# Chunk attention, Fourier mixing and an MLP on one core: pairs of batches in turn, or one batch at a time threaded through the MLP

## The chip, the cores and the metric

One core of a Trainium2 chip runs one program. Its engines work side by side, each through its own instructions in order: TensorE (PE in the rows; its weight loads are PEld), VectorE (DVE), ScalarE (ACT), GpSimd (POOL) and SyncE (SP), which here only issues DMAs. The metric is the time of one execution in microseconds of device time. TensorE's clock has two levels, 1.2 and 2.4 GHz; the profile tells the granted clock of a stretch as a share of the higher.

## The reference

Attention inside chunks of 64 tokens, then an FNet block: the real part of a Fourier transform over sequence and width is added to x, the sum u is normalised, and a two-layer MLP of the normalised rows is added back to u.

```python
# q, k, v: (8 batches, 8 heads, 576 tokens, 64), float32
scores = scale * np.matmul(q_c, k_c.transpose(0, 1, 2, 4, 3))   # chunks of 64
attn = np.exp(scores - max); attn = attn / (sum + 1e-09)
x = np.matmul(attn, v_c)        # -> (8, 576, 512) after the heads are joined
mixed = np.real(np.fft.fft(np.fft.fft(x, axis=1), axis=2))
u = x + mixed
un = (u - mean(u)) / np.sqrt(var(u) + 1e-06)
out = u + np.maximum(un @ w_ch1, 0.0) @ w_ch2      # 512 -> 2048 -> 512
```

The two weight matrices come as float64, and the kernel rounds them to float32 on the chip.

## The kernel before, in words

4608 rows make 36 tiles of 128 rows. A batch has nine chunks: four tiles of two chunks each (two of low chunks, `LO`, two of high ones, `HI`), and a middle chunk; the middle chunks of two batches share a tile (`RE`, "rest"). So the kernel works in four pairs of batches, nine tiles each.

A generator `attention(pr)` gives the attention of a pair in small steps, four to a tile: `att_S` (scores and their softmax, L215), `att_T` (transposes of q and k of the next tile, L197), `att_V` (probabilities times v, L252) and `att_P` (transposes of the probabilities, L246). `shift` (L282) moves single rows between tiles by DMA, `fold` (L296) adds and subtracts the low and high halves on GpSimd, which halves the Fourier work. `post(pr)` is the rest: the sequence transform (`z`, L368 and L378, into `zf`), the width transform (`mix`, L410) with u and its mean and variance (L423 to L429), the normalising (`un`, L440) and its transposes (`unT`), and the MLP in three groups of three tiles, 384 columns: `up` (L483) with the relu into `h` on ScalarE (L490), then `dn` (L501), the sum `o` (L512) and the store. TensorE takes a float32 matmul as two instructions, so that up is 128 instructions to a group and dn 96.

The order is written out by hand in the loop at the end. Attention of the first pair runs alone, with a weight piece rounded at every second step. Then `post` of a pair runs, and the steps of the next pair's attention are dealt out among its MLP steps, from the ninth step of `post` on; the Fourier part and the normalising of a pair stand between the MLPs of two pairs. A weight piece (32 of them, 128x512 float64, 512 KB) is rounded by seven operations on VectorE and a product on GpSimd (`round_weight`, L170), in place in one of two `raw` buffers; the load of piece i+2 is issued after the product of piece i. All DMAs are issued by SP, in order; a transfer's issue waits until the transfer eight before it has landed.

Of the kernel before, what the change touches and what calls it, by code (L numbers as in the profile page):

```python
# [16 lines left out]
def kernel(  # L17
# [45 lines left out]
    G = 3  # L63
    NG = NT // G
# [3 lines left out]
    in_p = ctx.enter_context(tc.tile_pool(name="in", bufs=3))  # L68
    one_p = ctx.enter_context(tc.tile_pool(name="one", bufs=1))
    two_p = ctx.enter_context(tc.tile_pool(name="two", bufs=2))  # L70
    sm_p = ctx.enter_context(tc.tile_pool(name="sm", bufs=4))
    x_p = ctx.enter_context(tc.tile_pool(name="x", bufs=2 * NT))
    pm_p = ctx.enter_context(tc.tile_pool(name="pm", bufs=2 * NM + 1))
# [6 lines left out]
    eps = const.tile([128, 1], FP32, name="eps")  # L80
    tk = const.tile([128, NM + 1, 2, NQ], FP32, name="tk")
# [5 lines left out]

    LO, HI, RE = "lo", "hi", "rest"
    order = [(RE, 0, 0)] + [(what, b, i) for b in range(2) for what in (LO, HI) for i in range(NM)]

    def kind(n):
        return order[n % NT][0]

    def chunks(n):

        pr, n0 = divmod(n, NT)
        what, b, i = order[n0]
        b += 2 * pr
        if what == RE:
            return [(2 * pr, NC // 2), (2 * pr + 1, NC // 2)]  # L100
# [7 lines left out]
    xs, pms = {}, {}  # L108

    def load(n):  # L110
        for src, dst, nm in ((q, qs, "q"), (k, ks, "k")):
            t = two_p.tile([128, H, D], FP32, tag=nm, name=nm)
            (b0, c0), (b1, c1) = chunks(n)
            if b0 == b1 and c1 == c0 + 1:
                parts = [(0, 128, b0, c0)]
            else:
                parts = [(0, CH, b0, c0), (CH, CH, b1, c1)]
            for p0, np_, b, c in parts:
                nc.sync.dma_start(
                    out=t[p0:p0 + np_], in_=src[b, :, c * CH:c * CH + np_, :].rearrange("h p d -> p h d")  # L120
                )
            dst[n] = t
        t = in_p.tile([128, 2, NJ, D], FP32, tag="v", name="v")
        for i, (b, c) in enumerate(chunks(n)):
            for e in range(2):
                nc.sync.dma_start(
# [5 lines left out]
    def load_tables():  # L132
# [4 lines left out]
        t = one_p.tile([128, NM + 1, 2, NQ], FP32, tag="big", name="seq")  # L137
# [3 lines left out]
        for r0 in (0, CH):  # L141
            nc.sync.dma_start(out=t[r0:r0 + 1, NM], in_=seq_tab[0:1, 0])
            nc.sync.dma_start(out=t[r0 + 1:r0 + CH, NM], in_=seq_tab[1:CH, NM])
        a, b = tk.rearrange("p i r f -> p (i r) f"), t.rearrange("p i r f -> p (i r) f")
# [4 lines left out]
        nc.sync.dma_start(out=cd, in_=dim_tab[:, 0:2, 0:HM + 1])  # L149
        nc.sync.dma_start(out=cs[:, HM + 1:DM], in_=dim_tab[:, 2, 1:HM])  # L150
        nc.sync.dma_start(out=sd, in_=dim_tab[:, 3, 1:HM])
        nc.gpsimd.memset(cs[:, 0:HM + 1], 0.0)
        nc.sync.dma_start(out=cs[0:1, 0:HM + 1], in_=dim_tab[0:1, 2, 0:HM + 1])
        nc.gpsimd.memset(cs[0:1, HM + 1:DM], 0.0)
# [6 lines left out]
    raws = {}  # L161

    def load_weight(i):

        if i < len(pieces):
            t = two_p.tile([128, 512, 2], U32, tag="raw", name="raw")
            nc.sync.dma_start(out=t.rearrange("p f r -> p (f r)"), in_=pieces[i][1].bitcast(U32))
            raws[i] = t

    def round_weight(i):  # L170

        if i >= len(pieces):
            return
        w, t = pieces[i][0], raws.pop(i)
        lo, hi, wi = t[:, :, 0], t[:, :, 1], w.bitcast(U32)
# [65 lines left out]
    def att_P(n):  # L245
        ex = es.pop(n)  # L246
        pt = turn(lambda j: ex[:, j].rearrange("p e k -> p (e k)"))
        t = two_p.tile([128, NJ, 128], FP32, tag="pT", name="pT")
# [3 lines left out]
    def att_V(n):  # L252
# [13 lines left out]
        x = x_p.tile([128, DM + 1], FP32, tag="x", name="x")  # L266
# [11 lines left out]
        xs[n] = x  # L278

    def tile_of(pr, what, b=0, i=0):  # L280
        return pr * NT + order.index((what, b, i))

    def shift(pr, b):

        lows = [xs[tile_of(pr, LO, b, i)] for i in range(NM)]
        r = b * CH
        rest = xs[tile_of(pr, RE)][r:r + 1, 0:DM]
        t = one_p.tile([2 * NM + 1, DM], FP32, tag="first", name="first")
        for i in range(NM):
            nc.sync.dma_start(out=t[2 * i:2 * i + 2], in_=lows[i][0:CH + 1:CH, 0:DM])  # L290
        nc.sync.dma_start(out=t[2 * NM:2 * NM + 1], in_=rest)
        for i in range(NM):
            nc.sync.dma_start(out=lows[i][0:CH + 1:CH, 0:DM], in_=t[2 * i + 1:2 * i + 3])
        nc.sync.dma_start(out=rest, in_=t[0:1])

    def fold(pr, b, i):  # L296

        pm = pm_p.tile([128, 2, HM], FP32, tag="pm", name="pm")
        if i == NM and b == 1:
            pms[pr, 1, NM] = pms[pr, 0, NM]  # L300
            return
        if i == NM:
            s = xs[tile_of(pr, RE)]
        else:
            s = sums[i]
            low, high = xs[tile_of(pr, LO, b, i)], xs[tile_of(pr, HI, b, i)]
            nc.gpsimd.tensor_tensor(out=s[:, 0:DM], in0=low[:, 0:DM], in1=high[:, 0:DM], op=ALU.add)
        near, far = s[:, 0:HM], s[:, DM:HM:-1]
        nc.gpsimd.tensor_tensor(out=pm[:, 0], in0=near, in1=far, op=ALU.add)
        if i < NM:  # L310
            near, far = far, near
        nc.gpsimd.tensor_tensor(out=pm[:, 1], in0=near, in1=far, op=ALU.subtract)
        mid = sm_p.tile([128, 1], FP32, tag="mid", bufs=2 * NM + 1, name="mid")
        nc.gpsimd.tensor_copy(mid, s[:, HM:HM + 1])
        pms[pr, b, i] = pm, mid

    def ready(pr, n):

        for b in range(2):
            for i in range(NM):  # L320
                if n == tile_of(pr, HI, b, i):
                    fold(pr, b, i)
            if n == tile_of(pr, LO, 1, NM - 1):
                fold(pr, b, NM)

    sums = [const.tile([128, DM + 1], FP32, name=f"sum{i}") for i in range(NM)]

    def attention(pr):

        first, last = pr * NT, (pr + 1) * NT - 1  # L330
        if pr == 0:
            load(0)
            load(1)
            load_tables()
            att_T(0)
        for n in range(first, last + 1):
            att_S(n)
            yield
            if n + 1 < NP * NT:
                att_T(n + 1)  # L340
            yield
            if n > first:
                att_V(n - 1)
                for b in range(2):
                    if n - 1 == tile_of(pr, LO, b, NM - 1):
                        shift(pr, b)
            if n + 2 < NP * NT:
                load(n + 2)
            yield
            att_P(n)  # L350
            ready(pr, n - 1)
            yield
        att_V(last)
        ready(pr, last)
# [3 lines left out]
    def post(pr):  # L358
        n0 = pr * NT
        zf = one_p.tile([128, 2, 4, NZ], FP32, tag="big", name="zf")  # L360
        for b in range(2):
            ins = [(*pms[pr, b, i], slice(0, 128), i) for i in range(NM)]
            ins.append((*pms[pr, b, NM], slice(b * CH, (b + 1) * CH), NM))
            for T in range(4):
                z = ps_f.tile([128, 512], FP32, tag="ff", name="z")
                fold_, half = T // 2, slice(T % 2 * 128, (T % 2 + 1) * 128)
                for pm, mid, p, i in ins:
                    nc.tensor.matmul(  # L368
                        out=z[:, 0:NQ],
                        lhsT=pm[p, fold_, half],  # L370
                        rhs=tk[p, i, fold_, :],
                        start=(i == 0),
                        stop=(i == NM),
                        skip_group_check=(T == 2),
                    )
                if T == 2:
                    for pm, mid, p, i in ins:
                        nc.tensor.matmul(  # L378
                            out=z[0:1, 0:NQ],
                            lhsT=mid[p],  # L380
                            rhs=tk[p, i, 0, :],
                            start=(i == 0),
                            stop=(i == NM),
# [214 lines left out]
```

## Time and profile before

| | |
|---|---|
| median of 3 runs | 1448.37 us (1448.15 to 1448.52) |
| profiled execution | 1449.68 us, its span 1447.9 us |
| mean granted clock | 0.935 |
| TensorE busy | 1287.3 us, 89% of the span |
| VectorE, ScalarE, GpSimd busy | 26%, 14%, 9% |
| read, written | 46.50 MB, 9.44 MB |

The page divides the span into 40 slices of 36.2 us and gives the busy tenths of each engine in each. In the chain that ended last, each step is followed back to what released it. A row of the chain is its start, its length and what ran. "x16" counts instructions that were merged into one row.

### The profile page before, as it was taken

The numbers are of one execution on the slowest core, as the hardware profiler recorded it, in microseconds if no ns is written. First come the engines' busy times: TensorE is split into PE (matmuls) and PEld (weight loads), VectorE is DVE, ScalarE is ACT, GpSimd is POOL, SyncE is SP. The second block draws the span as 40 slices with busy tenths as digits, with TensorE's granted clock in tenths as the row PEclk, the third lists the DMA queues.
The fourth block names the chain that finished last, engine by engine and source line by source line (L and its number), as shares of the span: only waits on it lengthen the run. The fifth ranks groups of instructions, "written<-read, shape, count | busy, mean of one in ns | idle before, by whom it ended". The sixth has DMA issues, their size and how long they took to land.

```text
span 1447.9 us, 14315 instructions
## 1 busy us (share of the span) xinstructions
PE 1287.3 (89%) x6000; PEld 698.2 (48%) x6000; DVE 381.4 (26%) x727; ACT 204.4 (14%) x443; POOL 131.2 (9%) x170
## 2 busy tenths in 40 slices
PE   3235859899999969999999959999999969999998
PEld 3223436455455446455455436455455435455553
DVE  3788687421111051121111051121111050000000
ACT  2010112012021022112021012112021011011010
POOL 0134122101001020001001020000001010000000
PEclk9556669999999989999999979999999989999999
DMA  6464224121110100021110101011100000000000
GB/s 155 103 148 108 73 69 121 45 52 28 39 45 15 37 15 22 15 52 25 42 44 16 37 15 23 15 38 37 39 14 7 16 1 0 10 13 8 15 0 22
DMA packets 126262, 57.03 MB, mean 39 GB/s; under 512 B 116533, under 2 KB 117046, under 8 KB 126198
## 3 DMA queue, kind: packets, MB, share of 16 engines
q1 hardware_dynamic: 126198, 56.13, 16.1%
q8 instruction: 47, 0.77, 0.2%
q14 instruction: 17, 0.14, 0.0%
HBM read 46.50 MB, written 9.44 MB: 39 GB/s over the span
## 4 chain that ended last, share of the span: by engine, by line
PE 81%; DVE 8%; issue 3%; POOL 3%; ACT 2%; DMA 2%; SPq 1%; POOLq 0%; DVEq 0%
PE up L483 35%; PE dn L501 34%; PE z L368 4%; PE pt L194 4%; POOL x L423 2%; PE xp L259 1%; PE sc L221 1%; PE mix L410 1%; DVE bst L425 1%; PE z L378 1%; DVE w L182 1%; DMA k<-in_k_dram 1%; DVE w L180 1%; DVE y L418 1%; DVE raw L186 1%
## 5 line engine op out<-in xcount | busy, mean ns | idle before, releaser
L483 PE MATMUL up<-unT,w 128*128 128x384 f32 x1536 | 517.1, 493 | 2.7 <-ACT unT L456 2.0
L501 PE MATMUL dn<-w,h 128*128 128x512 f32 x1152 | 504.5, 594 | 0.0
L483 PEld LDWEIGHTS up<-unT,w 128*128 128x128 f32 x1536 | 289.9, 192 | 196.4 <-issue 7.5
L501 PEld LDWEIGHTS dn<-w,h 128*128 128x128 f32 x1152 | 215.6, 190 | 256.0 <-issue 253.1
L490 ACT ACTIVATE h<-up 128x384 f32<-128x384 f32 x192 | 94.3, 491 | 512.0 <-PE up L483 512.0
L512 DVE TENSOR_TENSOR o<-dn,x 128x512 f32<-128x512 f32 x36 | 24.9, 692 | 396.7 <-PE dn L501 396.7
L230 DVE TENSOR_REDUCE mx<-sc 128x8 f32<-128x512 f32 x36 | 24.7, 687 | 242.7 <-PE sc L221 242.7
L194 PE MATMUL pt<-ident,q 128*128 128x128 f32 x144 | 27.1, 321 | 65.9 <-DMA q<-in_q_dram 65.9
L368 PE MATMUL z<-tk,pm 128*128 128x289 f32 (+1 forms) x192 | 69.5, 493 | 5.2 <-DVE zf L389 3.8
L194 PE MATMUL pt<-ident,un 128*128 128x128 f32 x144 | 25.4, 329 | 51.4 <-DVE un L440 49.4
L194 PEld LDWEIGHTS pt<-ident,q 128*128 128x128 f32 x144 | 20.5, 165 | 75.4 <-issue 72.8
L187 POOL TENSOR_TENSOR w<-w,raw 128x512 f32<-128x512 f32 x32 | 41.6, 1301 | 152.3 <-DVE raw L186 152.3
L268 DVE TENSOR_TENSOR x<-xp,rd 128x512 f32<-128x512 f32 x36 | 24.8, 690 | 115.5 <-PE xp L259 115.5
L368 PEld LDWEIGHTS z<-tk,pm 128*128 128x128 f32 (+1 forms) x192 | 35.5, 212 | 39.9 <-issue 28.0
L194 PEld LDWEIGHTS pt<-ident,un 128*128 128x128 f32 x144 | 20.2, 169 | 57.7 <-issue 41.7
L211 DVE COPY kT<-pt 128x512 f32<-128x512 f32 x36 | 24.5, 682 | 86.5 <-PE pt L194 86.5
L249 ACT COPY pT<-pt 128x512 f32<-128x512 f32 x36 | 21.1, 586 | 174.2 <-PE pt L194 174.2
L423 POOL TENSOR_TENSOR x<-y,x 128x513 f32<-128x513 f32 x16 | 27.4, 1711 | 189.6 <-DVE y L418 189.6
L440 DVE TENSOR_SCALAR un<-x,st,rstd 128x512 f32<-128x512 f32 x36 | 19.1, 558 | 94.3 <-PE pt L194 94.3
L238 ACT ACTIVATE ex<-ex 128x512 f32<-128x512 f32 x36 | 22.7, 629 | 143.9 <-DVE ex L232 143.9
L221 PE MATMUL sc<-kT,qT 64*64 64x64 f32 x1152 | 27.2, 237 | 14.9 <-ACT qT L204 13.6
L386 ACT COPY zf<-z 128x289 f32<-128x289 f32 x32 | 12.9, 402 | 183.2 <-PE z L368 151.0
(67 smaller groups left out, 682.1 us busy)
## 6 DMA issues: line engine op xcount, KB each, us to landing
raw<-in_moe_w_ch_dram SPq DMA_DIRECT2D x32, 512.0 KB
v<-in_v_dram SPq DMA_DIRECT2D x144, 64.0 KB
q<-in_q_dram SPq DMA_DIRECT2D x40, 128.0 KB
k<-in_k_dram SPq DMA_DIRECT2D x40, 128.0 KB
q<-in_q_dram SPq DMA_DIRECT2D x16, 256.0 KB
k<-in_k_dram SPq DMA_DIRECT2D x16, 256.0 KB
out_dram<-o SPq DMA_DIRECT2D x16, 256.0 KB
out_dram<-o SPq DMA_DIRECT2D x32, 128.0 KB
```

The source lines that it names most:

```text
L187: nc.gpsimd.tensor_tensor(out=w, in0=w, in1=lo.bitcast(FP32), op=ALU.mult)
L194: nc.tensor.transpose(pt[:, j, :], src(j), ident)
L211: nc.vector.tensor_copy(t, pt)
L221: nc.tensor.matmul(out=sc[t0:t0 + CH, e, j * CH:(j + 1) * CH], lhsT=a[r0:r0 + D, 2 * j + c, 0:CH], rhs=b[r0:r0 + D, j, t0:t0 + CH], start= ...
L230: nc.vector.tensor_reduce(out=mx, in_=s4, axis=AX.X, op=ALU.max)
L268: nc.vector.tensor_tensor(out=xo.rearrange("p (j e d) -> p e j d", j=NJ, e=2), in0=xp[:, :, 0:NJ * D].rearrange("p e (j d) -> p e j d", j=NJ),
L368: nc.tensor.matmul(out=z[:, 0:NQ], lhsT=pm[p, fold_, half], rhs=tk[p, i, fold_, :], start=(i == 0), stop=(i == NM), skip_group_check=(T == 2),
L423: eng.tensor_tensor(out=x[:, 0:w], in0=y[:, 0:w], in1=x[:, 0:w], op=ALU.add)
L483: nc.tensor.matmul(out=up, lhsT=w1[:, kk, m * 128:(m + 1) * 128], rhs=unT[:, kk, :], start=(kk == 0), stop=(kk == KD - 1),)
L490: nc.scalar.activation(out=h1[:, m, :], in_=up, func=ACTF.Relu)
L501: nc.tensor.matmul(out=dn, lhsT=h1[:, m, s * 128:(s + 1) * 128], rhs=w2[:, m, :], start=(m == 0), stop=(m == KF - 1),)
L512: nc.vector.tensor_tensor(out=o, in0=dn, in1=natural(n), op=ALU.add)
```

## The change

The work is cut by batch and not by pair: `attention(b)` and `fourier(b)` give one batch's steps, and both are dealt out among the steps of the MLP, as one sequence. MLP groups have four tiles (512 columns): one group for the four tiles of each batch, and a ninth for the four rest tiles at the end. The side steps of batch b+1 begin in the middle of the dn of batch b-1 and end in the middle of the dn of batch b, where the tiles of the next group are normalised and transposed between parts of dn. Attention and Fourier of batch 0 stand alone ahead of the first group.

Rounding a piece takes four operations on VectorE, three on ScalarE and the product on GpSimd, spread over two calls: call i does the first half of piece i and the second of piece i-1, and issues the load of piece i+2 into one of three buffers. Twelve calls stand in batch 0's attention and Fourier, the other 21 between the first fourteen up steps of group 0, two and one in turn. q and k of batch 0 are loaded ahead, k and half of v from ScalarE's queue. z and mix take their PSUM from the two buffers of the transposes (`ps_t`), not from those of the MLP. All x tiles lie in one constant tile `xall`.

```diff
+    groups = [[at[what, b, i] for what in (LO, HI) for i in range(NM)] for b in range(B)]
+    rests = [at[RE, b, 0] for b in range(0, B, 2)]
+    groups += [rests[i:i + G] for i in range(0, NP, G)]
...
+        for src, dst, nm, eng in ((q, qs, "q", nc.sync), (k, ks, "k", nc.scalar)):
+            if n < first[1]:
+                i = 2 * n + (nm == "k")
+                t = start[:, (4 + i) * DM:(5 + i) * DM].rearrange("p (h d) -> p h d", h=H)
...
+                eng = nc.scalar if n < first[1] and e else nc.sync
...
-        nc.vector.tensor_scalar(wi, hi, 0x000FFFFF, None, ALU.bitwise_and)
-        nc.vector.tensor_scalar(w, wi, 2.0 ** -20, 1.0, ALU.mult, ALU.add)
-        nc.vector.scalar_tensor_tensor(w, lo, 2.0 ** -52, w, ALU.mult, ALU.add)
-        nc.vector.tensor_scalar(lo, hi, 0x7FF00000, None, ALU.bitwise_and)
-        nc.vector.tensor_scalar(lo, lo, float(896 << 20), 0.0, ALU.subtract, ALU.max)
-        nc.vector.tensor_scalar(lo, lo, float(255 << 20), 8.0, ALU.min, ALU.mult)
-        nc.vector.scalar_tensor_tensor(lo, hi, 0x80000000, lo, ALU.bitwise_and, ALU.bitwise_or)
-        nc.gpsimd.tensor_tensor(out=w, in0=w, in1=lo.bitcast(FP32), op=ALU.mult)
-        load_weight(i + 2)
+        if i < len(pieces):
+            w, t = pieces[i][0], raw(i)
+            lo, hi, wi = t[:, :, 0], t[:, :, 1], w.bitcast(U32)
+            p = power[i] = three_p.tile([128, 512], U32, tag="o", name="power")
+            nc.vector.tensor_scalar(wi, hi, 0x000FFFFF, None, ALU.bitwise_and)
+            nc.scalar.activation(out=w, in_=wi, func=ACTF.Copy, scale=2.0 ** -20, bias=1.0)
+            nc.vector.tensor_scalar(p, hi, 0x7FF00000, None, ALU.bitwise_and)
+            nc.scalar.activation(out=p, in_=p, func=ACTF.Relu, scale=-1.0, bias=top[:, 0:1])
+            nc.scalar.activation(out=p, in_=p, func=ACTF.Relu, scale=-8.0, bias=top[:, 1:2])
+        if 0 < i <= len(pieces):
+            w, t = pieces[i - 1][0], raw(i - 1)
+            lo, hi = t[:, :, 0], t[:, :, 1]
+            p = power.pop(i - 1)
+            nc.vector.scalar_tensor_tensor(w, lo, 2.0 ** -52, w, ALU.mult, ALU.add)
+            nc.vector.scalar_tensor_tensor(p, hi, 0x80000000, p, ALU.bitwise_and, ALU.bitwise_or)
+            nc.gpsimd.tensor_tensor(out=w, in0=w, in1=p.bitcast(FP32), op=ALU.mult)
+            load_weight(i - 1 + len(RAWS))
...
+    def fourier(b):
+        h = b % 2
+        zf = one_p.tile([128, 4, NL], FP32, tag="zf", name="zf")
...
+            z = ps_t.tile([128, 512], FP32, tag="pt", name="z")
...
+            nc.scalar.copy(zf[:, T, :], z[:, 0:NL])
+            nc.scalar.copy(zr[:, h, T, 0:NQ - NL], z[:, NL:NQ])
...
+        for i in ((NM,) if h == 1 else ()) + tuple(range(NM)):
+            mix = ps_t.tile([128, 512], FP32, tag="pt", name="mix")
...
+                if m % (KF // PARTS) == KF // PARTS - 1:
+                    i = s * PARTS + m // (KF // PARTS)
+                    if g + 1 < NG:
+                        for j in range(G):
+                            if i == G * PARTS - 2 * (G - j) - 1:
+                                normed(g + 1, j)
+                            if i == G * PARTS - 2 * (G - j):
+                                turned(g + 1, j)
+                    if m < KF - 1:
                         yield
...
+        for _ in fourier(0):
+            round_weight(n_w)
+            n_w += 1
+        for s in range(G):
+            normed(0, s)
+            turned(0, s)
...
+        for g in range(NG):
+            for _ in mlp(g):
+                t += 1
+                if n_w <= len(pieces):
+                    for _ in range(2 if t % 2 else 1):
+                        round_weight(n_w)
+                        n_w += 1
+                if cur < len(sides):
+                    t0 = 12 if cur == 0 else N_READY + (cur - 1) * N_MLP
+                    t1 = N_READY + cur * N_MLP
+                    due = min(sizes[cur], (t - t0) * sizes[cur] // (t1 - t0 - 1))
+                    while done < due:
+                        next(sides[cur], None)
+                        done += 1
```

ScalarE's instructions at the very start: before, the cosine and sine tables (`tk`) are copied ahead of the first transposed q (`qT`).

```order
L524 ACT_TABLE_LOAD
L146 COPY tk<-seq 128x6x64 x4
L147 COPY tk<-seq 128x6
L148 COPY tk<-seq 128x6x32
L204 COPY qT<-pt 128x8x64
```

Of the change, the last of the DMA issues that now stand there, and what follows them:

```order
L175 DMA cs<-in_dim_tab_dram 128x255
L178 DMA cs<-in_dim_tab_dram 1x257
L146 DMA start<-in_k_dram 128x8x64
L156 DMA v<-in_v_dram 64x4x64 x2
L146 DMA start<-in_k_dram 64x8x64 x4
L246 COPY qT<-pt 128x8x64
L280 ACTIVATE ex<-ex 128x512
```

Twenty DMA issues have come in ahead of the first qT, and the table copies have gone to a place behind the third.

ScalarE during up: before, in a group of the first pair, the relu (`h`) alternates with a copy or exponential of attention now and then.

```order
L490 ACTIVATE h_1876<-up 128x384 x2
L238 ACTIVATE ex<-ex 128x512
L490 ACTIVATE h_1876<-up 128x384 x2
L204 COPY qT<-pt 128x8x64
L490 ACTIVATE h_1876<-up 128x384 x5
```

Of the change, at the beginning of group 0's up; `w_87` and `power` are the two parts of a weight piece being rounded:

```order
L541 ACTIVATE h_795<-up 128x512
L219 ACTIVATE w_87<-w_87 128x512
L221 ACTIVATE power<-power,top 128x512
L222 ACTIVATE power<-power,top 128x512
L219 ACTIVATE w_87<-w_87 128x512
L221 ACTIVATE power<-power,top 128x512
L222 ACTIVATE power<-power,top 128x512
L541 ACTIVATE h_795<-up 128x512
L219 ACTIVATE w_87<-w_87 128x512
L221 ACTIVATE power<-power,top 128x512
L222 ACTIVATE power<-power,top 128x512
L541 ACTIVATE h_795<-up 128x512
```

Between two relus stand three or six operations of the rounding.

TensorE behind the dn of a group: before, between two pairs, the whole z and mix of the next pair follow it in one piece.

```order
L501 MATMUL dn<-w_93,h_2312 128x512 x32
L368 MATMUL z<-tk,pm 128x289 x9
L378 MATMUL z<-tk,mid 1x289 x3
L368 MATMUL z<-tk,pm 128x289 x12
L378 MATMUL z<-tk,mid 1x289 x3
L368 MATMUL z<-tk,pm 128x289 x3
```

Of the change, in the dn of group 1:

```order
L546 MATMUL dn<-w_88,h_1760 128x512 x8
L411 MATMUL z<-tk,pm 128x289 x2
L411 MATMUL z<-tk,pm_rest 128x289
L546 MATMUL dn<-w_88,h_1760 128x512 x4
L411 MATMUL z<-tk,pm 128x289 x2
L411 MATMUL z<-tk,pm_rest 128x289
L546 MATMUL dn<-w_88,h_1760 128x512 x4
```

Each step of z has a part of dn (four matmuls) on either side.

## Rows read from the trace of the kernel before

**Rows 1.** Page: engines' busy time, TensorE's busy tenths and clock in 40 slices.

```profile
PE 1287.3 (89%) x6000; PEld 698.2 (48%) x6000; DVE 381.4 (26%) x727; ACT 204.4 (14%) x443; POOL 131.2 (9%) x170
...
PE   3235859899999969999999959999999969999998
...
PEclk9556669999999989999999979999999989999999
```

**Rows 2.** Windows: start:end, length, busy us by engine (instructions), PEclk, DMA share, GB/s.

```profile
0.00:205.00 205.00, 96.50 (x852) 60.31 (x852) 142.64 (x268) 29.28 (x67) 53.77 (x64) 0.67 0.44 109
...
10.00:20.00 10.00, 0.00 (x0) 0.00 (x0) 0.00 (x0) 1.82 (x6) 0.30 (x1) 1.00 0.82 207
35.00:148.00 113.00, 44.86 (x520) 29.14 (x518) 91.99 (x161) 12.79 (x23) 37.09 (x40) 0.58 0.49 120
148.00:165.00 17.00, 16.70 (x30) 7.09 (x30) 8.51 (x19) 1.21 (x3) 3.85 (x3) 0.50 0.32 93
515.00:535.00 20.00, 8.00 (x57) 5.38 (x56) 15.80 (x35) 3.91 (x16) 6.84 (x4) 0.74 0.12 26
```

**Rows 3.** Chain that ended last: start us, us, what ran.

```profile
20.29 0.49 ACT qT L204
...
205.01 13.42 PE up L483 x32
...
815.62 5.36 PE z L368 x18
...
833.52 3.24 PE mix L410 x13
...
841.80 1.72 POOL x L423
...
846.39 1.72 POOL x L423
...
865.07 12.78 PE up L483 x32
...
934.18 0.44 PE pt L194 x4
...
941.48 0.63 PE sc L221 x32
...
1235.14 41.20 PE dn L501 x96
1276.35 41.30 PE up L483 x128
...
1443.16 0.69 DVE o L512
```

**Rows 4.** Timeline, TensorE: mix of a rest tile, then of two others.

```profile
507.26 1.08 PE L410 MATMUL mix<-cd,zf 128*64 128x257 f32 x4
...
510.49 1.14 PE L410 MATMUL mix<-cd,zf 128*128 128x257 f32 x4
...
512.75 1.03 PE L410 MATMUL mix<-cd,zf 128*128 128x257 f32 x4
```

**Rows 5.** Lines by form: busy us, mean ns | idle before, releaser.

```profile
L230 DVE TENSOR_REDUCE mx<-sc 128x8 f32<-128x512 f32 x36 | 24.7, 687 | 242.7 <-PE sc L221 242.7
...
L307 POOL TENSOR_TENSOR sum<-x 128x512 f32<-128x512 f32 x16 | 21.0, 1314 | 1.3
```

**Rows 6.** Tile raw: duration ns min/median/max, first and last start; last row idle us.

```profile
L180 DVE TENSOR_SCALAR w<-raw x32: 375/418/1449, 35.6 to 269.8; 128x512 uint32<-128x512 uint32 x32
L182 DVE SCALAR_TENSOR_TENSOR w<-raw,w x32: 691/693/1639, 36.5 to 270.7; 128x512 f32<-128x512 uint32 x32
...
  DMA raw<-in_moe_w_ch_dram: 2.7, 4
```

**Rows 7.** Timeline: a weight load issued, and the operation that waited for it.

```profile
214.87 24.32 SPq L167 DMA_DIRECT2D raw<-in_moe_w_ch_dram  x5
...
218.97 0.43 DVE L180 TENSOR_SCALAR w<-raw 128x512 uint32<-128x512 uint32 x1 [1.60 <-DMA raw<-in_moe_w_ch_dram]
```

More of the change, by code (lines that the diff above doesn't have):

```diff
@@ L277, in att_V, with shift @@
             nc.gpsimd.memset(x[:, DM:DM + 1], 0.0)
[L278 to L288, printed above, removed]
+    def shift(b):
+        lows = [xt(at[LO, b, i]) for i in range(NM)]
+        r = b % 2 * CH
+        rest = xt(rests[b // 2])[r:r + 1, 0:DM]
+        t = three_p.tile([128, XW], FP32, tag="y", name="first")
@@ L296, in fold @@
[L296 to L303, printed above, removed]
-        else:
[L305 to L309, printed above, removed]
+            nc.sync.dma_start(out=lows[i][0:CH + 1:CH, 0:DM], in_=t[2 * i + 1:2 * i + 3, 0:DM])
@@ new lines, in shift, with fold @@
+        nc.sync.dma_start(out=rest, in_=t[0:1, 0:DM])
+    def fold(b, i):
+        if i < NM:
+            pm = two_p.tile([128, 2, HM], FP32, tag="pm", name="pm")
+            mid = sm_p.tile([128, 1], FP32, tag="mid", name="mid")
+            s = three_p.tile([128, XW], FP32, tag="y", name="sum")
+            low, high = xt(at[LO, b, i]), xt(at[HI, b, i])
+            nc.gpsimd.memset(s[:, DM:DM + 1], 0.0)
+            nc.gpsimd.tensor_tensor(out=s[:, 0:DM], in0=low[:, 0:DM], in1=high[:, 0:DM], op=ALU.add)
+            p = slice(0, 128)
+        else:
+            if b % 2 == 0:
+                pm = one_p.tile([128, 2, HM], FP32, tag="pm_rest", name="pm_rest")
+                mid = sm_p.tile([128, 1], FP32, tag="mid_rest", bufs=2, name="mid_rest")
+            else:
+                pm, mid, _ = pms[b - 1, NM]
+            s = xt(rests[b // 2])
+            p = slice(b % 2 * CH, (b % 2 + 1) * CH)
+        near, far = s[p, 0:HM], s[p, DM:HM:-1]
+        nc.gpsimd.tensor_tensor(out=pm[p, 0], in0=near, in1=far, op=ALU.add)
@@ L310, in fold @@
         if i < NM:
             near, far = far, near
[L312 to L319, printed above, removed]
-            for i in range(NM):
[L321 to L334, printed above, removed]
+        nc.gpsimd.tensor_tensor(out=pm[p, 1], in0=near, in1=far, op=ALU.subtract)
+        nc.gpsimd.tensor_copy(mid[p], s[p, HM:HM + 1])
+        pms[b, i] = pm, mid, p
+    def attention(b):
+        lo, hi = first[b], first[b + 1] - 1
+        def ready(n):
+            if n == at[LO, b, NM - 1]:
+                shift(b)
+            for i in range(NM):
+                if n == at[HI, b, i]:
+                    fold(b, i)
+            if n == at[HI, b, 0]:
+                fold(b, NM)
+        if b == 0:
@@ L335, in attention @@
             att_T(0)
-        for n in range(first, last + 1):
+        for n in range(lo, hi + 1):
             att_S(n)
             yield
-            if n + 1 < NP * NT:
+            if n + 1 < NT:
                 att_T(n + 1)
+                if n + 3 < NT and n + 3 >= first[1]:
+                    load(n + 3)
             yield
-            if n > first:
+            if n > lo:
                 att_V(n - 1)
[L344 to L348, printed above, removed]
-            yield
-            att_P(n)
-            ready(pr, n - 1)
-            yield
@@ L353, in attention @@
-        att_V(last)
-        ready(pr, last)
-        yield
[L358 to L366, printed above, removed]
+                if n + 2 < NT:
+                    load_v(n + 2)
@@ L375, in post @@
                     )
[L376 to L383, printed above, removed]
-                            skip_group_check=True,
-                        )
-                nc.scalar.copy(zf[:, b, T, 0:NQ], z[:, 0:NQ])
@@ L398, in post @@
             if i == NM:
[L399 removed]
+                parts = [(j * CH, CH, zr[:, j]) for j in range(2)]
             else:
[L401 removed]
+                parts = [(0, 128, zf[:, :, 128 * i:128 * (i + 1)])]
             for p0, np_, zt in parts:
```

350 lines of the change are left out of this document (191 added, 159 removed).

## The prediction, made before the changed kernel was run

> **What bounds the kernel now.** I read the page first: TensorE is busy 89% of the span, and its row of tenths shows where it isn't, the first five or six slices and three dips about 330 us apart; the granted clock sinks at the same places [rows 1]. Between them it works without a gap at full clock. Then the windows: up to 205 us, when the first MLP begins, TensorE is busy 96.5 us and VectorE 142.6; from 35 to 148 us it is VectorE that is full (92.0 of 113), with attention of nine tiles and weight rounding in one queue, and TensorE, busy 44.9, has a clock of 0.58 [rows 2]. Then the chain, for the dips: z of the second transition starts at 815.62 and the next up at 865.07, 49.5 us, of which TensorE works about 30; the rest goes along POOL and VectorE, one mix every 4.6 us (841.80 to 846.39) [rows 3]. So the MLP is bound by TensorE, the start by VectorE, the dips by the chain from mix to un. The change can gain only in the last two, and I work it out as the time to the first MLP, a slow group 0, and TensorE's remaining work without gaps.
>
> **To the first MLP (now 205 us).** *Loads.* The last k load stands ahead of the first qT on ScalarE's queue, and its issue waits for the transfer eight before it. Ahead of that lie nine q, k, v tiles of 256 KB and 1.4 MB of tables, 3.8 MB. SP alone moves 207 GB/s between 10 and 20 us [rows 2], so 18 us, and with 2 to 3 us before the first byte qT comes at 22, against 20.29 now [rows 3]. Queued behind these issues is everything of ScalarE, and TensorE's scores wait for it. If two queues moved a quarter more it would be 18; if ScalarE's issues cost more than SP's, 26.
> The Trainium skill ("DMA: Bandwidth & Descriptors", section "Issuing engines are not separate DMA queues") says that DMAs of several engines run on the same 16 DMA engines, and a second issuer saves only issue time. The DMA engines are 0.82 busy in that window with one issuer, which agrees; by issue time alone qT would come near 14, and the total would be 8 us less.
> *Attention of batch 0.* A tile costs VectorE five operations like mx, 0.69 each [rows 5], and two small ones: 3.9 us, about 5 with the exponential and copies between (an estimate). Two and a half tiles from 22, and the table copies now in the middle of ScalarE's queue (2.3), bring the first rounding call to about 36. A whole call costs VectorE two masks (0.42 each) and two combining operations (0.69 each) [rows 6], 2.4 with gaps; the maxima of the same rows are 2.4 and 3.5 times the medians, so I take 3.0 here, where GpSimd folds beside it. From the first call to the last value product: half a call, four whole ones and two and a half tiles, 0.9 + 12 + 9.7, and 4 of ScalarE's latency: 62. The last fold on GpSimd (sum 1.31 [rows 5], two half-wide operations, and the product queued ahead of it) ends at 66.
> *Fourier of batch 0.* z of one batch is 30 instructions, 16.7 us at the clock of 0.50 from 148 to 165 [rows 2]: 81. The first mix at that clock, 4.5: 85.5. Then the chain of two mixes, 4.6 each, with a call of 3.2 behind each: 101. Four tiles of un, transposes and copies: 106. Bounds: 92, if z runs at full clock (9 us) and the calls at 2.4; 120, if each call costs what the old seven operations do (3.8 and more).
>
> **Group 0 (up among 21 rounding calls).** Call i issues load i+2 at its end, and call i+2 begins with that piece; between them lies one call. A load takes 4.1 us from issue to use (214.87 to 218.97 [rows 7]); a call keeps VectorE 2.4 to 3.0, say 2.7. So two periods are 2.7 + 4.1, and a call comes every 3.4 us: the split of the work, four operations for seven, gains less than it seems, since the load sets the pace. Between two relus ScalarE has one or two calls' operations, which wait for VectorE's, and up has two PSUM buffers: TensorE can't run more than two steps ahead. An up step of 512 columns is 8 instructions like dn's, 41.20 / 96 = 0.429 each [rows 3], 3.43 us; one and a half calls are 5.1. Batch 1's first probabilities, behind the fourteenth step, wait for the softmax, which is queued behind 20 calls on VectorE: 20 x 3.4 + 2.5 = 70.5, and 2 for a clock that isn't up at once (the first 32 of up took 13.42 at 205 us, 12.78 at 865, and a quarter of the 41.30 of a whole group, 10.3, at full clock [rows 3]). So these probabilities are transposed at 106 + 72.5 = 178.5. ScalarE isn't the limit: its mean instruction is 0.46 us [rows 1], a call three of them. Bounds for the call: 2.7 (the load hidden, 20 calls 54) and 4.3 (loads 5.9, queued behind each other; 86).
>
> **What TensorE then still has to do**, all durations from rows at full clock:
> - MLP: 9 groups x 256 instructions x 0.429 = 988.8, less 14 steps done, 48.0: 940.8. 512 columns in place of 384 change nothing per column: 41.30 / 128 is 0.323, 4/3 of it 0.430 [rows 3].
> - Attention: pt of q, k and the probabilities 0.44 each, scores and values 0.63 each [rows 3]: 2.58 a tile, 31 tiles, less 2.4 already done: 77.6. Transposes of un: 32 x 0.44 = 14.1.
> - z: 815.62 to 833.52 is two batches, 8.95 each [rows 3]; 7 batches: 62.7.
> - mix: 2.26 a tile pair (510.49 to 512.75), 3.23 the rest tile (507.26 to 510.49) [rows 4]: 14 x 2.26 + 4 x 3.23 = 44.5.
>
> Sum 1139.7. These now stand between parts of dn or up of 3.43 us, so that what VectorE, ScalarE and GpSimd do for the next step lies beside MLP work: this hides the copies of z (now two on ScalarE), the halved rest folds and added memsets on GpSimd, the un operations, the later q, k, v loads and shift's DMAs (asked for two tiles ahead). The mix chain of 4.6 us has 3.43 + 2.26 = 5.7 between two mixes, and about 6.9 before the first transposed un. z's first step comes one part after the last values; VectorE's 0.69 and the fold's 3 are 3.7 to 4, against 3.43 and the first third of z: half a microsecond late, seven times. In group 0 the side steps come two at a time and three mixes in a row, some 3 late. I allow 10 for waits in all (3 to 25).
>
> **The end.** From the last dn (the last o starts at 1443.16 [rows 3]) to the span's end is 4.7 now; a rest tile stores with four transfers in place of two: 5.8.
>
> **Sum:** 178.5 + 1139.7 + 10 + 5.8 = 1334. This is a span; the profiled execution takes 1449.68 for its 1447.9, and the median of the runs is 1.3 below it, so that a median lies 0.5 above the span: 1334 us (rounded), 114 less than now.
>
> **Rivals.**
> 1. *Rounding isn't held by loads* (chance 0.15). For it: before, only 4 of 32 pieces waited for a load, 2.7 us in all [rows 6], and buffers are three now. Against it: those two buffers had far more time between calls. The pace is then VectorE's, 2.7, 14 less, and the start some 10 less: 1310.
> 2. *A cold, longer group 0* (0.22). TensorE gets 3.43 us of work in each 5.1, and the window of 515 to 535, 8 us busy of 20, shows 0.74 [rows 2]; window 148 to 165 stays at 0.50 although TensorE is busy 16.7 of 17. At the lower clock an up step is 6.9 us, 14 steps 96 in place of 72: 24 more, with calls and start a little longer: 1365. Against it: at 0.50 it is always busy, and the first up at 205 rose within its first 32 instructions.
> The Trainium skill ("TensorE: Matmul & The Clock Gate", section "HAM oscillation — how this bites in real kernels") has it that repeated short waits between bursts make the clock fall again and again; the dip's 0.74 agrees. By that rule alone the time is the one of this rival.
> 3. *The Fourier steps stall TensorE in every batch* (0.05): slower. TensorE takes its queue in order, and some 45 of the 170 side steps are z or mix, which share two PSUM buffers with all transposes and wait for ScalarE and VectorE; none of them has stood inside an MLP so far. It decides from 2.5 us per step on: 45 x 1.5 us more of waiting gives 68, and a clock of 0.50 for 17 us behind each of 7 batches 60 more: 1334 + 128 = 1462. Against it: the attention steps of now stand among MLP pieces without a gap, and the chain of a mix is shorter than its spacing.
> That the gaps only move, and nothing is gained (within 0.2%), I give 0.01; it would need the start to stay near 205.
>
> **Chances and range.** My forecast, with 1315 to 1350 around it, 0.57. Low end: start 14 less, calls 14 less, waits 6 less: 1300. High end: start 14 more, group 0 24 more, waits 12 more: 1384. I give 1300 to 1383. 0.2% is about what a measurement of this kernel can tell from no change: faster by more 0.93, within 0.02, slower 0.05.
>
> **What would show it.** Right: first up at 100 to 112 us; calls 3.2 to 3.7 us apart in group 0, with VectorE's first mask waiting for the load, and up's steps about 5 us apart there; the first transposed probabilities of batch 1 near 178; from then on PE without gaps at clock 1.0 and a group of 125 to 130 us with its side steps; dn's end 6 us before the end. Wrong: gaps of over 2 us around each z or mix, a clock under 0.9 after 200 us, or a first up later than 125 us.

## The result, and the profile after

The changed kernel takes 1344.94 us, median of 4 runs (1344.15 to 1346.33), against 1448.26 for the kernel before on the same chip. The ratio is 0.9289, 95% interval 0.9273 to 0.9305. The forecast was 1334, with 1300 to 1383 around it. The profiled execution took 1346.33 us, its span 1344.5.

The page of the changed kernel, same lines as [rows 1]:

```profile
PE 1262.8 (94%) x5616; PEld 610.3 (45%) x5616; DVE 338.2 (25%) x639; ACT 253.7 (19%) x517; POOL 133.5 (10%) x196
...
PE   2468879999999999999999999999999999999998
...
PEclk9667989999999999999999999999999999999999
```

The three dips are gone, in the tenths and in the clock. What is left stands in the first six slices of 33.6 us. The windows, with the columns of [rows 2]: the start, z in it, group 0 up to the first transposed probabilities of batch 1, and everything behind.

```profile
0.00:108.90 108.90, 51.06 (x450) 32.42 (x451) 52.67 (x112) 39.94 (x77) 27.88 (x40) 0.75 0.65 139
65.00:85.00 20.00, 17.51 (x50) 7.22 (x42) 10.43 (x20) 9.25 (x18) 8.08 (x10) 0.50 0.46 133
...
108.90:178.30 69.40, 55.91 (x153) 23.89 (x153) 57.53 (x83) 46.72 (x76) 25.68 (x21) 0.89 0.45 144
178.30:1344.50 1166.20, 1155.79 (x5014) 553.99 (x5014) 227.96 (x446) 167.09 (x365) 79.97 (x136) 1.00 0.12 27
```

The chain that ended last, to be laid beside [rows 3]:

```profile
24.73 0.60 ACT qT L246
...
69.24 9.55 PE z L411 x16
...
85.33 3.54 PE mix L454 x8
...
108.91 6.70 PE up L534 x8
...
180.73 4.89 PE up L534 x8
...
190.75 0.44 PE pt L236 x4
191.19 0.62 PE sc L263 x32
191.81 3.63 PE dn L546 x8
195.44 0.87 PE pt L236 x8
196.32 0.62 PE xp L301 x32
...
368.56 1.66 PE z L411 x6
370.22 3.63 PE dn L546 x8
373.85 2.16 PE mix L454 x8
376.00 3.43 PE dn L546 x8
...
1229.82 54.93 PE up L534 x128
...
1339.73 0.69 DVE o L564
```

The first up stands at 108.91 (205.01 before). From 190 us on the chain is TensorE's alone but for a few places: parts of dn or up alternate with side steps. Compare the parts: eight instructions take 3.63 us behind the scores (`sc`), behind the values (`xp`) and behind a step of z, and 3.43 behind a mix. Most of what the prediction had too small is this difference, as shown below.

### The profile page after: what moved, and what is told of

Same layout as the page of the kernel before. It is cut to its first block, busy times and chain, and to the rows that moved or that the text cites. A ratio compares the mean times of both kernels' runs of the same rounds, so it can differ in the third digit from the quotient of the medians.

```text
span 1344.5 us, 13655 instructions
## 1 busy us (share of the span) xinstructions
PE 1262.8 (94%) x5616; PEld 610.3 (45%) x5616; DVE 338.2 (25%) x639; ACT 253.7 (19%) x517; POOL 133.5 (10%) x196
## 4 chain that ended last, share of the span: by engine, by line
PE 87%; DVE 5%; DMA 5%; ACT 1%; POOL 1%; issue 1%; SPq 0%; ACTq 0%; POOLq 0%; DVEq 0%
PE dn L546 37%; PE up L534 34%; PE z L411 4%; PE pt L236 4%; PE mix L454 3%; DMA xall<-in_moe_w_ch_dram 2%; PE sc L263 2%; PE xp L301 1%; PE z L421 1%; DVE w L218 1%; DMA start<-in_q_dram 1%; DMA start<-in_k_dram 1%; DVE power L228 1%; DVE unT L503 1%; POOL xall L469 1%
## 5 line engine op out<-in xcount | busy, mean ns | idle before, releaser
L534 PE MATMUL up<-unT,w 128*128 128x512 f32 x1152 | 520.2, 602 | 7.1 <-ACT h L541 6.2
L534 PEld LDWEIGHTS up<-unT,w 128*128 128x128 f32 x1152 | 214.2, 192 | 253.5 <-issue 240.1
L541 ACT ACTIVATE h<-up 128x512 f32<-128x512 f32 x144 | 85.8, 596 | 440.7 <-PE up L534 440.6
L564 DVE TENSOR_TENSOR o<-dn,xall 128x512 f32<-128x512 f32 x36 | 24.8, 690 | 248.4 <-PE dn L546 248.4
L310 DVE TENSOR_TENSOR xall<-xp,rd 128x512 f32<-128x512 f32 x36 | 24.9, 691 | 120.6 <-PE xp L301 120.6
L469 POOL TENSOR_TENSOR xall<-y,xall 128x513 f32<-128x513 f32 x16 | 27.6, 1726 | 260.4 <-DVE y L462 260.4
L229 POOL TENSOR_TENSOR w<-w,power 128x512 f32<-128x512 f32 x32 | 41.1, 1284 | 89.1 <-DVE power L228 89.1
L411 PE MATMUL z<-tk,pm 128*128 128x289 f32 x128 | 41.6, 449 | 2.5 <-POOL pm L355 2.5
L253 DVE COPY kT<-pt 128x512 f32<-128x512 f32 x36 | 24.7, 686 | 49.8 <-PE pt L236 49.8
L411 PEld LDWEIGHTS z<-tk,pm 128*128 128x128 f32 x128 | 25.6, 206 | 23.1 <-issue 15.0
L301 PE MATMUL xp<-v,pT 64*64 64x64 f32 x1152 | 26.3, 232 | 8.3 <-ACT pT L291 8.3
```

The source lines that it names most:

```text
L229: nc.gpsimd.tensor_tensor(out=w, in0=w, in1=p.bitcast(FP32), op=ALU.mult)
L301: nc.tensor.matmul(out=xp[t0:t0 + CH, e, j * D:(j + 1) * D], lhsT=a[r0:r0 + CH, j, t0:t0 + CH], rhs=b[r0:r0 + CH, c, j, :], start=True, st ...
L310: nc.vector.tensor_tensor(out=xo.rearrange("p (j e d) -> p e j d", j=NJ, e=2), in0=xp[:, :, 0:NJ * D].rearrange("p e (j d) -> p e j d", j=NJ),
L411: nc.tensor.matmul(out=z[:, 0:NQ], lhsT=pm[p, fold_, half], rhs=tk[p, i, fold_, :], start=(i == 0), stop=(i == NM), skip_group_check=(T == 2),
L469: eng.tensor_tensor(out=x[:, 0:w], in0=y[:, 0:w], in1=x[:, 0:w], op=ALU.add)
L534: nc.tensor.matmul(out=up[:, 0:cols], lhsT=w1[:, kk, m * 128:(m + 1) * 128], rhs=unT[:, kk, 0:cols], start=(kk == 0), stop=(kk == KD - 1),)
```

## The experiments

All ratios are to the kernel before, on the same chip as each run.

**Threading alone taken back** (`block`). The Fourier part, the normalising and the transposes of a batch run as one block between two groups; attention is still dealt out among MLP steps, and the rounding, the loads and the start are those of the change.

```diff
-            yield from fourier(b)
...
+                if g + 1 < B:
+                    for _ in fourier(g + 1):
+                        pass
+                for s in range(G):
+                    normed(g + 1, s)
+                    turned(g + 1, s)
```

> The changed kernel with the steps of Fourier, normalising and transposing of a batch taken out of the MLP and put as one block between two groups; attention stays dealt out, the start stays as it is. If the dips are what the threading removes, each of the seven block places costs the chain of two or three mixes (4.6 us each, of which TensorE works half), the four tiles of un, transposes and copies one after another (about 6 us), and a lower clock behind it (2 to 3 us): 12 to 16 us each, with 5 for the rest group: 1345 + 90 to 115 = 1435 to 1460, which is the time before, so that threading is the whole gain. Rival (the gain lies in the shorter start and the batch-wise cut, the dips being cheap): under 1400.

Measured: 1447.64 us, 0.9992 (0.9983 to 1.0001). Its page and two groups of its lines, behind 178 us (busy us, mean ns | idle before, releaser):

```profile
PE   2469799699989999799979997999979997999998
...
PEclk9559999899998999799989998899989998999999
```

```profile
L534 PE MATMUL up<-unT,w 128*128 128x512 f32 x1032 | 473.4, 614 | 7.0 <-DVE unT L503 7.0
...
L236 PE MATMUL pt<-ident,un 128*128 128x128 f32 x128 | 29.3, 406 | 67.3 <-ACT rstd L476 55.3 <-DVE un L492 12.0
```

Seven dips show behind the first slices, one for each transition, where before there were three, with a lower clock beside them; TensorE waits 67.3 us for the normalised tiles ahead of their transposes, where the change leaves 1.5, and its mean clock is 0.939 against 0.972. First up (110.50) and first probabilities of batch 1 (179.21) are as early as in the change. So without the threading nothing is gained: a start that is 95 us earlier is paid back where each single batch has its own transition. The expected range held it, and the rival, a time under 1400, falls. What the shorter start alone would give with the old cut by pairs, which has only three transitions, no run shows.

**The old rounding in the new schedule** (`oldround`): seven operations on VectorE and the product on GpSimd in one call, three buffers.

```diff
-            nc.scalar.activation(out=w, in_=wi, func=ACTF.Copy, scale=2.0 ** -20, bias=1.0)
-            nc.scalar.activation(out=p, in_=p, func=ACTF.Relu, scale=-1.0, bias=top[:, 0:1])
-            nc.scalar.activation(out=p, in_=p, func=ACTF.Relu, scale=-8.0, bias=top[:, 1:2])
+            nc.vector.tensor_scalar(w, wi, 2.0 ** -20, 1.0, ALU.mult, ALU.add)
+            nc.vector.tensor_scalar(lo, lo, float(896 << 20), 0.0, ALU.subtract, ALU.max)
+            nc.vector.tensor_scalar(lo, lo, float(255 << 20), 8.0, ALU.min, ALU.mult)
```

> The new schedule with the old rounding: seven VectorE operations per piece and the GpSimd product in the same call, the load of piece i+3 issued after call i; ScalarE has no part in it. Theory (the split with ScalarE is a small part of the gain, and it works through the first group only, since all rounding lies in the first 180 us): a call costs about 4.0 us of VectorE (0.42 + 0.69 x 3 + the shorter ones) in place of the 3.15 measured with the split, the first up product comes 8 to 10 us later than 108.9, the first probabilities of batch 1 some 20 to 25 us later than 178.3, and the time is 1360 to 1372. After that nothing differs. Rival (the loads set the pace of the calls anyway, as they wait on every load): within 5 us of 1344.9, calls still 3.2 us apart.

Measured: 1381.69 us, 0.9538 (0.9524 to 0.9552), 10 us above the range of the theory. The first up comes at 118.8, as expected; but the first probabilities come at 213.6, 35.3 later than in the change, since a call takes 4.67 us. Timeline of a call (start, length, engine, line; in brackets the idle time before it and its releaser):

```profile
127.28 1.40 DVE L218 TENSOR_SCALAR w<-w 128x512 f32<-128x512 uint32 x1
128.71 0.69 DVE L219 SCALAR_TENSOR_TENSOR w<-xall,w 128x512 f32<-128x512 uint32 x1
...
131.96 1.39 DVE L218 TENSOR_SCALAR w<-w 128x512 f32<-128x512 uint32 x1
...
126.99 1.40 POOL L224 TENSOR_TENSOR w<-w,xall 128x512 f32<-128x512 f32 x1 [3.21 <-DVE xall L223]
```

The conversion on line 218 lasts 1.40 and ends at 128.68, 0.29 after GpSimd's product (128.39), while the like operations on lines 220 to 222 take 0.43. One operation of VectorE, the one which meets the product, lasts as long as the product does. The theory was right about the place (behind the first probabilities TensorE is busy 1155.3 us, for 1155.8 in the change), and too low by 0.7 us a call; the rival, that loads set the pace anyway, falls.

**Five raw buffers in place of three** (`raws5`).

```diff
-    RAWS = [2 * G, 2 * G + 2, NR + 1]
+    RAWS = [2 * G, 2 * G + 2, NR + 1, G, G + 2]
```

> The changed kernel with five raw weight buffers in place of three, nothing else. My theory: in group 0 the load sets the pace of the rounding calls, since a piece is asked for only one call ahead of its use (VectorE's first mask waits for the load at every second call, a pair of calls takes 6.3 us). With five buffers it is asked for three calls ahead: no waits for loads in group 0, calls 2.6 to 2.8 us apart, batch 1's first probabilities transposed at about 168 in place of 178, and the time 8 to 12 us less: 1335. Rival (VectorE, ScalarE or the DMA engines set the pace themselves): the waits go, but calls stay over 3 us apart, and the time stays within 3 us of the changed kernel's 1344.9.

Measured: 1338.85 us, 0.9242 (0.9229 to 0.9254). The waits for loads are gone and the probabilities come at 171.60, but calls are 2.96 us apart, and the time is 4 us above the 1335 of the theory; it is 6 us below the change, where the rival had at most 3. First the change, then this kernel, in group 0:

```profile
128.62 1.18 DVE L218 TENSOR_SCALAR w<-xall 128x512 uint32<-128x512 uint32 x1 [0.46 <-DMA xall<-in_moe_w_ch_dram]
129.72 0.41 DVE L220 TENSOR_SCALAR power<-xall 128x512 uint32<-128x512 uint32 x1
...
131.58 1.39 DVE L218 TENSOR_SCALAR w<-xall 128x512 uint32<-128x512 uint32 x1 [0.25 <-DMA xall<-in_moe_w_ch_dram]
...
128.25 1.27 POOL L229 TENSOR_TENSOR w<-w,power 128x512 f32<-128x512 f32 x1 [1.90 <-DVE power L228]
```

```profile
124.45 0.41 DVE L218 TENSOR_SCALAR w<-xall 128x512 uint32<-128x512 uint32 x1
124.79 1.49 DVE L220 TENSOR_SCALAR power<-xall 128x512 uint32<-128x512 uint32 x1
...
127.41 0.42 DVE L218 TENSOR_SCALAR w<-xall 128x512 uint32<-128x512 uint32 x1
...
124.61 1.39 POOL L229 TENSOR_TENSOR w<-w,power 128x512 f32<-128x512 f32 x1 [1.56 <-DVE power L228]
```

In the change a call waits 0.2 to 0.6 us for its load, and its first mask, begun beside the product, lasts 1.18. Without the wait the first mask begins ahead of the product and gets through, and the second one meets the product: 1.49, again to 0.28 past its end. Two limits lay on top of each other, the load at 3.15 us a call and GpSimd's product at 2.96.

Not all of the gain lies in group 0. The first up already comes 2.1 us earlier (106.8 for 108.9), for in the change one call in the attention of batch 0 waits long for its load, and with five buffers it doesn't:

```profile
61.32 0.48 DVE L218 TENSOR_SCALAR w<-xall 128x512 uint32<-128x512 uint32 x1 [4.70 <-DMA xall<-in_moe_w_ch_dram]
```

**All loads from SP** (`spq`).

```diff
-        for src, dst, nm, eng in ((q, qs, "q", nc.sync), (k, ks, "k", nc.scalar)):
+        for src, dst, nm, eng in ((q, qs, "q", nc.sync), (k, ks, "k", nc.sync)):
...
-                eng = nc.scalar if n < first[1] and e else nc.sync
+                eng = nc.sync
...
```

The six issues of the tables on ScalarE's queue go to SP in the same way.

> The changed kernel with all loads of batch 0 and the tables issued from SP, none from ScalarE. My theory of the start: ScalarE's first copy (qT) comes late, at 24.7 us, because 20 DMA issues stand ahead of it in ScalarE's queue and each waits for the transfer eight before it. Without them qT is copied when q is transposed, before 10 us; the first tiles' attention then runs beside the loads, the first rounding call waits for its weights alone and comes some 3 to 6 us earlier, and so does the first MLP: 1339 to 1342. Rival (two issuing queues bring the loads in sooner, which is worth more): the loads land later by several us, the first rounding call and the first MLP with them, 1348 or more. Rival (the bytes alone decide): no change within 1 us.

Measured: 1339.42 us, 0.9246 (0.9233 to 0.9258). The first copy of ScalarE, in the change (with the DMA issues ahead of it) and in this kernel:

```profile
19.97 4.71 ACTq L146 DMA_DIRECT2D start<-in_k_dram  x4
24.73 0.59 ACT L246 COPY qT<-pt 128x512 f32<-128x512 f32 x1 [22.71 <-DMA start<-in_k_dram]
```

```profile
6.05 0.59 ACT L246 COPY qT<-pt 128x512 f32<-128x512 f32 x1 [4.04 <-PE pt L236]
```

In the change TensorE had transposed the first q and k by 9.1 us, and the copy stood behind ScalarE's own DMA issues until 24.73; here it comes at 6.05. Of these 18.7 us the first up gets back 5.7 (103.19 for 108.91): the chain now goes along SP's issues, and then waits for a weight piece, behind all other loads, which lands at 33.1. Both rivals fall, as the time is 5.5 us lower and neither the same nor higher.

**Values directly behind scores** (`sv`): the value products of the tile before stand in the same step as the scores, so that one break of the MLP per tile falls away. **Scores and values each with transposes behind them** (`pairs`): the step of the scores ends with the transposes of the next q and k, that of the values with those of the probabilities.

```diff
             att_S(n)
+            if n > lo:
+                att_V(n - 1)
...
             yield
             if n + 1 < NT:
                 att_T(n + 1)
```

```diff
             att_S(n)
-            yield
             if n + 1 < NT:
                 att_T(n + 1)
...
                 ready(n - 1)
-                yield
             att_P(n)
```

> The changed kernel with the value product of the tile before (att_V) put right behind the scores (att_S) in one step, the number of steps unchanged. My prediction's working left out that a part of up or dn (8 instructions) takes 3.63 us behind scores, values, z or the rest mix, and 3.44 us behind transposes: 0.19 us of a weight load not hidden, behind each step that uses half the rows or columns of the array, some 90 times. If that is the missing term, one of the two such places of a tile goes: 31 x 0.19 = 6 us less, 1339. Rival (the 0.19 is only how the profile places the ends of matmuls, and costs nothing): no change within 1 us, and the missing time is somewhere else. Rival (values now wait for the copied probabilities): 1 to 3 us more per batch, 1350 or more.

> One edit: the transposes of q and k stand in the same step directly behind the scores, and the transposes of the probabilities directly behind the values, so that a part of up or dn never follows scores or values; the number and place of the steps stays (two of four are empty). Theory (a part of up or dn takes 3.63 us behind scores or values and 3.44 behind transposes, 0.19 more, 62 times): -11.8 us, 1331 to 1335, and in the chain nearly no part of 3.63 behind scores or values is left. Rival A (each place where attention breaks the MLP costs the same whatever stands there; 31 places fewer gave -7.9 us, 62 fewer give -16): 1327 to 1330. Rival B (the 7.9 us came from values and folds that were done earlier, and not from TensorE): within 3 us of 1344.9.

Measured: `sv` 1337.05 us, 0.9229 (0.9217 to 0.9242), 2 us better than expected; `pairs` 1335.37, 0.9213 (0.9198 to 0.9228). The chain of `sv`:

```profile
324.38 0.47 PE xp L301 x32
324.85 3.63 PE up L535 x8
328.48 0.87 PE pt L236 x8
329.35 6.87 PE up L535 x16
```

The part behind the values still takes 3.63, but behind the transposes, where in the change the values stand between two parts, the two together take 6.87, 3.44 each. In the chain the parts of up and dn together are 5.6 us shorter, and the value products 2.8 (0.47 for 0.62 where they follow the scores directly), for they now stand behind matmuls of their own shape; TensorE's busy time behind the first probabilities falls from 1155.8 to 1147.0. So the 0.19 is no mere matter of how the profile places ends, and both rivals fall. TensorE's weight loads in the change point at the place:

```profile
191.74 0.30 PEld L546 LDWEIGHTS dn<-w,h 128*128 128x128 f32 x2
...
194.85 0.14 PEld L236 LDWEIGHTS pt<-ident,q 128*128 128x128 f32 x1 [0.24 <-issue]
```

Behind the scores dn's first load begins at 191.74, together with its first matmul (191.75); behind dn the first load of the transposes begins 0.43 us ahead of their matmuls (195.28). That the lost time is this load is read from these rows; no run changes the load alone.

In `pairs` the time lies 0.4 us above the theory's range, and comes about in another way. Its chain:

```profile
188.07 0.63 PE sc L263 x32
188.70 1.02 PE pt L236 x8
189.72 3.44 PE dn L547 x8
193.16 0.62 PE xp L301 x32
193.78 0.59 PE pt L236 x4
```

The parts of dn are 3.44 now, but the transposes behind scores or values have grown by 0.15 (0.87 to 1.02, 0.44 to 0.59): the loss has moved to them. Busy time falls by 4.5 only (to 1151.35). The rest of the 11.3 by which the span is shorter is an earlier group 0 (first up at 105.8 for 108.9, probabilities at 175.2 for 178.3) and 3.8 us less waiting behind it, 3.1 of it that of the transposes of k for the copy of a transposed un:

```profile
L236 PE MATMUL pt<-ident,k 128*128 128x128 f32 x116 | 17.9, 277 | 3.1 <-DVE unT L503 3.1
```

This row is the change's; in `pairs` the same group shows no idle time. Rivals A and B fall with the time.

**Three edits together** (`abc`: `raws5`, `spq` and `sv`), **the same with the product on VectorE** (`abcv`), and **that with the order of `pairs` in place of `sv`'s** (`best`).

```diff
-            nc.gpsimd.tensor_tensor(out=w, in0=w, in1=p.bitcast(FP32), op=ALU.mult)
+            nc.vector.tensor_tensor(w, w, p.bitcast(FP32), ALU.mult)
```

> Three edits in one: five raw buffers in place of three, all loads issued from SP, and the value products of the tile before put directly behind the scores in one step. Alone they gave -6.1, -5.5 and -7.9 us. Theory (three different places: the loads' wait in group 0, ScalarE's start, the joints of attention and MLP): they add up, 1322 to 1328; first up at 102 to 104, first probabilities of batch 1 at 163 to 167, remainder after that 1158. Rival (the first two are one wait seen from two sides): 1329 to 1333.

> As the kernel with the three edits, and the rounding's last product on VectorE in place of GpSimd. With five raw buffers the mask of the exponent (line 220) took 1.38 us in place of 0.52, and the GpSimd product 1.57 in place of 1.28. Theory (the two slow each other down when they run at the same time): with the product on VectorE at about 0.69 the mask falls to about 0.4, a call is 0.42 + 0.40 + 0.68 + 0.68 + 0.69 = 2.9 us against 2.96 with GpSimd, and the time is within 3 us of the kernel with the three edits. Rival (the mask is slow by itself): a call of 3.85 us, first probabilities some 12 us later, time 8 to 13 us above the kernel with the three edits.

> Five raw buffers, all loads from SP, the rounding's last product on VectorE, and the pairing of scores with transposes and of values with transposes in place of scores with values. The kernel with the first three and scores with values took 1322.1. Theory (0.19 us at 31 places more): 1315 to 1318. Rival (the pairing delays something at the start, where attention stands alone with the rounding): 1320 to 1326.

Measured: `abc` 1326.40 us, 0.9156 (0.9142 to 0.9170): 18.5 of the sum of 19.5, so the three places are separate. `abcv` 1322.10, 0.9126 (0.9110 to 0.9141). In its timeline the mask is short again and a call takes 2.60 us, less than the 2.9 expected, since operations of one engine overlap by about 0.08 each:

```profile
128.66 0.42 DVE L218 TENSOR_SCALAR w<-xall 128x512 uint32<-128x512 uint32 x1
129.00 0.42 DVE L220 TENSOR_SCALAR power<-xall 128x512 uint32<-128x512 uint32 x1
...
130.65 0.69 DVE L229 TENSOR_TENSOR w<-w,power 128x512 f32<-128x512 f32 x1
131.26 0.42 DVE L218 TENSOR_SCALAR w<-xall 128x512 uint32<-128x512 uint32 x1
```

VectorE does more work and is done sooner: the probabilities of batch 1 come at 162.5 for 166.4 of `abc`. The time is 4.3 us lower, a little outside the 3 expected; the rival, that the mask is slow by itself, falls. `best` 1321.92, 0.9120 (0.9107 to 0.9134), against 1315 to 1318 expected: the pairing is worth no more than `sv`'s order (TensorE is busy 1152.0 us behind the first probabilities, for `abcv`'s 1146.9, and waits 4 us less). The time lies in the range of the rival, but what the rival named for it did not happen, as its first up (102.4) is no later than `abcv`'s (103.1). `abcv` and `best` can't be told apart; both beat the changed kernel by 1.7%.

## Why the prediction was right, and where its terms were off

Its sum, in spans: 178.5 + 1139.7 + 10 + 5.8. Measured: 178.3 + 1155.8 + 5.6 + 4.8. The mechanism held, and one term of it was mis-sized. That 178.5 met 178.3 is luck: the first MLP came 2.9 us late, and group 0 was 3.1 us shorter.

- **To the first MLP**: 106 forecast, 108.9 measured. qT came at 24.7 and not 22, the first rounding call at 40.8 and not 36, and z began at 69.2 and not 66; on the way lies the wait of 4.70 us for a weight load, which the sum did not have. z ran at 0.50 as taken over, and ended at 85.3 for 81: it took 16.1 us, and the sum had allowed 15 where its own row says 16.7. The bound of 26, ScalarE's issues costing more than SP's, was the right warning; `spq` shows the price, 5.5 us in the time.
- **Group 0**: 69.4 us against 72.5. The load set the pace, as said, with a call every 3.15 us (eight from 122.44 to 147.60) for 3.4. Rival 1 was half there: `raws5` shows the load to be worth 6 us, not 14, for GpSimd's product stood right behind it as the next limit; 2.1 of the 6 lie ahead of group 0. I had put the long maxima of [rows 6] down to GpSimd's folds and spread them over a call as 3.0 for 2.4. For the combining operation (1639 ns) that holds: its four long runs all overlap a fold. For the mask (1449 ns) it doesn't: its twelve long runs all overlap a product, which here comes with every call.
- **TensorE's work, 1139.7, is the mis-sized term**: 16.1 too small. I had priced the attention steps at their own durations and every part of up or dn at 3.43, as in a run of 32 or 128 of them. Where such a part follows scores or values it takes 3.63; there are 61 such places behind 178 us, 30 of scores and 31 of values, at 0.19 each 11.6 us. `sv` takes away half of them and gives that half back, and more. Parts behind z or the rest mix take 3.63 too, at 29 places of the chain, 5.5 us; but the steps of z and mix themselves are shorter than I had priced them (in the batch of the rows above z takes 8.26 us for 8.95, a mix 2.16 for 2.26), by about as much. Some 2 us are the low clock up to 185 us: the part at 180.73 takes 4.89. The remaining 2 to 3 I can't assign to rows.
- **Waits**: 5.6 for 10, tail 4.8 for 5.8. z and mix stall TensorE nowhere behind 250 us; rival 3 did not happen. The row for it is the mix of 2.16 at 373.85, with 3.43 of dn behind it and no idle time.
- **Rival 2**, a cold, longer group 0, did not happen either, though the clock did swing: 0.89 over group 0, with 0.67 from 105 to 120 us and 1.00 from 120 to 135. From 165 to 180 us it was 0.77, with TensorE busy 6.8 us of 15. TensorE was busy 55.9 of 69.4 us, and from 118 us on the chain of group 0 runs along loads and VectorE, so the rounding set the length. The Trainium skill ("TensorE: Matmul & The Clock Gate", section "HAM oscillation — how this bites in real kernels") says that short waits between bursts let the clock fall again; the trace agrees with that. What the low clock cost here is 3.3 us in the first step of up (6.70 at 108.91, for 3.43) and the 2 us up to 185.
- **The split of the rounding** is worth more than "gains less than it seems": in the new schedule 36.7 us (1381.69 to 1344.94). The gain of 103 is the threading's in the sense that without it none is left (`block`), and a third of it also needs the split.
- **The dip** of 49.5 us before the change holds 34.8 us of TensorE's work and not about 30; the figure enters no term of the sum.

## What to carry to other kernels

Price a small step that is cut into a stream of matmuls with its neighbours: what the next large matmul loses by it belongs to the step. Before calling one wait the pace of a loop, look for the limit just behind it; five buffers took 6 us where the load alone promised more. And if a compute engine issues DMAs, its own first operation waits behind all issues that stand ahead of it.

## What the runs showed of the hardware

- **A mask or conversion of VectorE that begins while a GpSimd product runs is held until the product ends**: 0.41 becomes 1.49, 0.43 becomes 1.40, and one that began ahead of the product isn't held (0.41 at 124.45 in `raws5`); with the product on VectorE it is 0.42 again and the call falls from 2.96 to 2.60 us. The Trainium skill ("SBUF — State Buffer", section "Who interferes with whom") states it: the two engines share a pair of ports under an exclusive lock, which a fast `tensor_scalar` takes, and the later one blocks. The trace agrees; the masks and conversions held here are of that kind.
- **A switch between matmuls that use half the array (scores and values 64*64, the rest's z 64*128, its mix 128*64) and full ones costs 0.15 to 0.19 us**, at whichever instruction comes first behind it: a part of dn (3.63 for 3.43), transposes (0.59 for 0.44), or the value products behind full ones (0.62 for 0.47). Between matmuls of one kind it isn't seen.
- **DMA issues hold up the engine that makes them**: four issues took 4.71 us on ScalarE, and its first copy, 6.05 us into the program without them, came at 24.73. An issue alone takes about 0.63 (SP in `spq`); the rest is waiting for earlier transfers to land, which the program asks for.
